# The skip term of eight tiles by VectorE into PSUM, identity or addition chosen per state tile, and a new order list

## The chip, the core and the metric

The kernel runs on one core of a Trainium2 chip. The metric is the device time of one execution in microseconds (us), lower is better; several runs are made and their median is given. The engines are named as in the profile: PE is TensorE (PEld its weight loads), DVE is VectorE, ACT is ScalarE, POOL is GpSimd, and SP (SyncE) issues DMA transfers.

## The reference

Two branches over the same 2048 rows of 512 columns are mixed by a gate g per row, g = sigmoid(sum(x * gate_w)):

```python
# branch a: a diagonal complex state-space scan, with a skip term
Bu = einsum("bld,pd->blp", x, B_bar)
for t in range(L): h = Lam_bar * h + Bu[:, t, :]
a = 2.0 * einsum("blp,dp->bld", hseq, Cmat).real + x * Dskip
# branch b: linear attention, 32 heads of 16, softmax(+) and softmax(-) features
num = phi_q @ (phi_k^T v);  den = phi_q @ sum(phi_k) + 1e-6
b = (num / den) @ wo
out = g * a + (1 - g) * b
```

The skip term x * Dskip is an elementwise product: a row of x times one vector of 512 numbers.

## The kernel before

The 2048 rows are split by residue modulo 8: row number = (a * 128 + c) * 8 + r, with r from 0 to 7, two halves a, and 128 rows c. So there are 16 output tiles of 128 rows, numbered ti = 2r + a; the list `order` has tile n of the output loop take r in the order 7, 1, 3, 5, 0, 2, 4, 6. x stands transposed in SBUF (`xT`), loaded by DMA transposes.

The stages are small generators, and every `yield` ends one step. A list, `ORDER`, written out by hand or by a planner, names the steps in the order in which they are issued, and PE, DVE, ACT and SP keep that order. A token is a stage with a tile number (`y4`), with `@` the PSUM banks it takes, with `:D` that its PSUM copy or scaling goes to DVE instead of ACT, with `:A` that its store is issued by ACT instead of SP. POOL is not in that manual schedule. Its instructions follow in program order, each behind its own waits.

The stages that matter here:

- `k`, `v`, `q` (L477 to L491): projections of x, by products on PE at L475, copied to SBUF by `evac` (L119 on ACT, L121 on DVE).
- `x`, `n`, `e`, `s` (features of k; `X`, `N`, `E`, `S` for groups 1 to 3 of q, `xA` to `sA` for group 0): trees of maxima and minima on DVE (L511, L521, L527), exponentials on ACT (L138), sums on DVE, a factor `rho`, and DMA transposes from SP into `phT` (L563).
- `g` (L597): products of x with B, 256 columns each (L601), and with powers of the decay (L606, L608), copied to `uv`.
- `z` and `h` (L622, L660): the scan over 256 chunks gives the state at r = 7 (`H7`); `st_h(r, j)` makes the states of the other r for state tile j (four tiles). There `dg` times the earlier state goes into PSUM (L668), and `uv` is added in one of two ways: by a product with the identity into the same bank (L667) and a copy by `evac`, or by an addition on DVE out of PSUM (L672). Which one is set by `H_VECTOR`, L54: r = 1, 2, 4, 5, 6 are added on DVE, r = 0 and 3 by the identity.
- `c` (L586 to L619): the scaled output matrices `C2r`, `C2i`, of which `phT0` is the scratch.
- `y` (L711): for one output tile, eight products of 512 columns with C2 (L717, four per step), then four products of 128 columns with a diagonal matrix `Dd` that holds Dskip (L722). They stay in one PSUM bank, `py`.
- `o` (L725): attention for one tile: products `pn` (L736), logarithm and copy `nu`, `rd` on ACT, the product `on` on DVE (L744), and its transposition to `oT`: by a DMA transpose from SP (L758), or for the last four tiles on PE (L753).
- `t` (L761): four products with Wo into the same bank `py` (L765), the scaling by the gate into `ot` (L769 on ACT, L771 on DVE), and the store (L773).

`END` (L696) closes the memory pools of the first part and opens those of the last.

Of the kernel before, what the change touches and what calls it, by code (L numbers as in the profile page):

```python
# [23 lines left out]
ORDER = """
NR F:28 NI B W1@0 W0@1 W0 W2@2 W1:D W3@3 W3 f1@4 W2:D f0@5 f2@6 f0 f1:D l10 V@0 F:4 V P f3@1 f3 f2:D F:4 P P k1@2 k1
l13 P2 k0@3 P2 U P2 P2 P2 P2 P4 k2@4 P3 P3 k3@5 P4 P4 k0 v0@0 i0 i2 U i0 i0 i1 i2 k4@7 i0:D i0 k2 i2 i2:D i2 U k3 k5@6
i1 v3@1 n0 x0 l9 i1 V2@2 i3 l12 x0 k4 v2@3 i3 i3 l14 i1 k5 n0 x0 n0 x0 i3 k7@4 n0 x0 U n0 i1 l11 k6@5 n1 x1 x1 n1 x1
n1 l8 R0 R1 x1 i3 k7 M v7@7 x1 n1 n1 k6:D L V2 v1@6 x2 n2 e0 v6@4 v5@5 v4@2 e0 x2 s0 v0 l15 n2 s0 n2 v2 s0 v1 R2 s0 v6
v3 n2 k10@0 k10 s0 k9@3 k9 C4 k13@6 gw D R3 s0 k12@4 e1 v7 s0 e1 s1 C6 k11@1 k11 x2 s1 k14@0 k8@3 k12 k14 k8 v4 k13
a0@71 a0 x2 s1 x2 s1 v5 g00@4 g00 g60@0 n2 x3 s1 g20@3 g60 s1 g10@2 g10 n3 e2 g30@6 g40@5 g10 s1 a1 x3 g20 n3 a1 x3 n3  # L30
x3 g41@4 n3 C3 e2 e2 e2 x3 g30 g40 g30 k15@0 k15 n3 e3 s2 x4 s2 x4 g01@2 g01 e3 e3 s2 g50@3 g11@5 g50 s2 s2 s2 n4 x4
n4 Q3 n4 s2 g50 g21@6 e3 s3 v8@0 g31@2 g11 Q2 g11 n4 g70@3 Q1 s3 C7 g21 g70 v9@5 g70 g70 z0 z0 g31 g31 Q0 w1@6 C0 a2
a2 a2 w0@3 s3 z0 v11@2 v9 g61@5 g41 R4 z0 w1 v8 z0 z0 g61 s3 w2@4 s3 s3 a2 x4 z0 z0 g51@6 g51 x4 w2 C2 s3 w3@0 g51 v11
n4 R5 w3 g71@5 g71 g71 g71 z1 z1 g02@4 g02 g42@6 a3 a3 z0 z0 g42 w0 e4 e4 z1 z1 z1 g62@2 g12@0 q1@5 C1 h50@4 C5 J1 e4
e4 z1 q2@6 q2 g12 g12 g22@3 g22 J0 h50 z1 z1 g62 q3@4 q3 J2 s4 z1 s4 q0@6 z1 s4 q0 q1 xA nA g32@0 J3 g32 g32 h60@3 J0
g52@2 g52 c4 h60 J2 c4 g52 h51@4 c2 s4 s4 g72@6 R7 g72 xA h10@5 nA g72 g72 c2 xA J3 nA h10 v10@0 v10 J1 s4 c5 h51 c5
R6 g23@3 v12@2 c4 c0 c0 g63@5 nA z2 z2 a3 a3 g03@4 xA g03 z2 z2 z2 z2 xA g23 z2 z2 g33@6 c5 v12 z2 z2 g13@0 g13 g63
g43@4 h32@3 g13 nA g43 h52@2 h52 g33 h32 h61@5 h61 h12@0 c0 g53@4 h12 g33 g53 s4 v14@3 c2 eA eA h42@2 h42 g73@6 g53 eA
eA g73 g73 q10@5 sA h11@0 h11 O h00@4 g73 sA v13@2 h00 v13 a4 z3 sA v15@6 z3 v15 h20@0 h01@4 h30@2 v14 h20 sA h30 z3
h31@6 z3 z3 sA a4 h01 h31 c6 c6 sA q13@3 q13 z3 a4 a4 Y Y h22@0 G q10 z3 z3 G q6@2 q6 h22 z3 z3 sA sA Y Y c1 c1 q9@4  # L40
q8@6 q5@7 h62@3 h41@5 c3 h41 c1 c3 c3 h13@0 h62 q11@2 h13 q11 q8 q12@1 c6 q12 h21@5 q5 h21 h02@2 c7 q4@6 q4 h53@3 h53
h23@1 h23 h33@0 h33 sA q9 h40@7 h40 sA q7@5 h43@6 h63@3 c7 h43 q7 c7 y4@0 y4 sA h63 sA h03@1 END h02 o0@4 o0 X1 N1
o1@7 o1 q14@6 X1 N1 h03 o0@5 X1 o1@2 o1 o1 o0 o0 q15@3 o2@4 o2 o2@7 o2 N1 q15 X1 N1 X1 N1 E1 E1 y2@1 y1@2 y1 E1 E1 q14
X2 y0@5 y0 o1 y4 X2 N2 X2 o0 o0 o3@4 o3 o3@7 o3 o1 o3 y2 X2 N2 o2 X2 N2 S1 S1 N2 S1 o3 S1 N2 S1 S1 o3 y5@3 o2 o2 S1 S1
S1 y1 E2 E2 E2 E2 y9@6 G N3 y5 y5 y3@4 y2 X3 X3 N3 t1 G t1 N3 S1 N3 S2 y9 y9 S2 S2 S1 S1 S2 y3 y3 t3 y0 t0 t0 t2 t2
y6@7 X3 t2:A o4@2 o4 o4@5 o4 o4 y6 y6 t3 X3 o4 X3 o4 S2 S2 t3 o5@1 o5 o5@2 o5 o5 y13@5 y13 o5 N3 o6@4 S2 o6 o6@1 o6 o6
y12@2 o5 y7@4 y7 y12 o6 o6 t4 y7 S2 S2 t4:D S2 E3 E3 E3 E3 S2 o7@1 o7 t5 t5 S3 o7@0 o7 S3 o7 t6 S3 o7 S2 o7 y8@1 o8@3
t6 o8 o8@0 o8 o8 S3 S3 y12 t0:A y11@7 o8 o8 o9@3 o9:D o9@0 o9:D S3 y8 y8 o9 o9 S3 S3 o9 o10@3 y11 o10 o10@0 y11 o10
o10 S3 y14@3 S3 y14 t7 t7:D t8 y14 t8 y15@0 o11@4 S3 o11 o11@1 t9 o12@4 o11:D o11 S3 o10 o10 o12 o12@1 o12 o12 t9:D
o11 y15 o13@4 o13:D o13@6 t6:A o13 o13 o11 o12 y10@1 o14@4 y15 o14:D o12@6 t9 o12:D t7:A t1 y10 y10 o13 o15@4 o15  # L50
o15@6 t4:A t5 o15 o15 t8 o15 t12 t12 t12:A t10 o14@4 o14 o14 t10:D o13@6 t11 o15@2 o15 t10 o13:D t11 t11:A y13 t13 o14
o14@1 t15 t15 t15 o14:D t14 t13 t13 t14 t14:A
"""
# [15 lines left out]
def kernel(  # L69
# [589 lines left out]

    def st_h(r, j):  # L660
        ph = bank([P, 2, NC], F32, "ph")
        add = (r, j) in H_VECTOR
        for h in range(2):
            t = 2 * j + h
            src = hs(r - 1, t, slice(0, NC)) if r in (2, 4, 6) else hs(7, t, slice(-1, NC - 1))
            if not add:
                MM(out=ph[:, h, :], lhsT=ident[:], rhs=uv[j][:, r, h, :], start=(h == 0), stop=False, skip_group_check=True)  # L667
            MM(out=ph[:, h, :], lhsT=dg[:, (r + 1) // 2 if r % 2 else 0, t, :], rhs=src, start=(add and h == 0), stop=True, skip_group_check=True)  # L668
        yield
        dst = HM[:, 2 * j:2 * j + 2, (r - 1) // 2, :] if r % 2 else HE[r // 2][:, 2 * j:2 * j + 2, :]  # L670
        if add:
            VT(out=dst, in0=ph[:], in1=uv[j][:, r], op=ALU.add)  # L672
# [38 lines left out]
    def st_y(n):  # L711
        ti = order[n]
        r, a = ti // 2, ti % 2
        py = bank([P, D], F32, "py")
        live["py", n] = py
        for t in range(NT2):
            MM(out=py[:], lhsT=hs(r, t, slice(a * P, (a + 1) * P)), rhs=C2B[t], start=(t == 0), stop=False)  # L717
            if t % 4 == 3:
                yield
        for kt in range(KT):  # L720
            xs = xT[:, kt, ti * P:(ti + 1) * P]
            MM(out=py[:, kt * P:(kt + 1) * P], lhsT=xs, rhs=Dd[:, kt, :], start=False, stop=False)  # L722
# [38 lines left out]
    def st_t(n):  # L761
        ti = order[n]
        py, oT = live["py", n], live["oT", n]
        for g in range(HG):
            MM(out=py[:], lhsT=oT[:, g, :], rhs=Wo[:, g, :], start=False, stop=(g == HG - 1))  # L765
        yield
        ot = pools["op"][1].tile([P, D], BF16, name="ot", bufs=14)
        if sel["eng"] == "act":
            nc.scalar.mul(out=ot[:], in_=py[:], mul=G[:, ti:ti + 1])  # L769
        else:  # L770
            VS(out=ot[:], in0=py[:], scalar1=G[:, ti:ti + 1], scalar2=None, op0=ALU.mult)  # L771
# [76 lines left out]
```

## Time and profile before

| | before |
|---|---|
| median of 3 runs (lowest to highest) | 155.52 us (155.03 to 155.8) |
| profiled execution, first to last instruction (the one time that the page gives for it) | 153.2 us |
| PE busy | 146.2 us (95%) |
| DVE busy | 132.4 us (86%) |
| ACT busy | 129.2 us (84%) |
| POOL busy | 15.8 us (10%) |
| bytes moved by DMA | 17.55 MB |

Busy time is the union of an engine's instructions. Rows of groups read: line, engine, operation, output and inputs, shape, count, then busy us, mean ns of one, and idle us ahead of the group with what ended it. Rows of stages read: stretch, length, then busy us and count for PE, PEld, DVE, ACT and POOL, the granted clock, the DMA share (1 is all 16 DMA engines), GB/s. Rows of the timeline read: start, length, engine, line, operation, with `x` and a count where equal instructions are merged. Rows of waits read: who waited, for whom, us in total, times, longest. DMA rows end in the median us from issue to landing.

### The profile page before, as it was taken

How to read it: one execution, taken by the hardware profiler on the slowest of the kernel's cores; microseconds unless marked ns; L12 is line 12 of the kernel's file. 1: busy time of each engine (PE TensorE's matmuls, PEld its weight loads, DVE VectorE, ACT ScalarE, POOL GpSimd, SP SyncE). 2: the span in 40 equal slices, each digit the busy share in tenths (PEclk: the TensorE clock that was granted, in tenths of full speed). 3: DMA queues.
4: the chain of work that ended last, by engine and by line, in shares of the span. 5: the costliest groups of instructions: out<-in, count | busy, mean ns of one | idle time of the engine just before them, and what ended most of it. 6: DMA issues, size and time to landing. Idle time of an engine off the chain costs nothing.

```text
span 153.2 us, 3361 instructions
## 1 busy us (share of the span) xinstructions
PE 146.2 (95%) x1236; PEld 95.0 (62%) x1254; DVE 132.4 (86%) x303; ACT 129.2 (84%) x279; POOL 15.8 (10%) x43
## 2 busy tenths in 40 slices
PE   7899999999999999999999999999999999999990
PEld 7644434788878985869867656555554455555540
DVE  3799999999999999999999999999999958717520
ACT  3489998999998999999998999699498998627562
POOL 8239980000000000000000000000000000000000
PEclk9999999999999999999999999999999999999997
DMA  4875995534445699930000007711278859969842
GB/s 116 164 218 97 223 178 112 103 75 103 103 107 78 129 230 178 166 115 4 0 0 4 0 0 169 74 37 34 42 98 147 176 122 189 162 129 206 247 143 103
DMA packets 50848, 17.55 MB, mean 115 GB/s; under 512 B 44176, under 2 KB 50832, under 8 KB 50832
## 3 DMA queue, kind: packets, MB, share of 16 engines
q1 hardware_dynamic: 48976, 15.75, 53.8%
q10 hardware_dynamic: 1696, 1.57, 3.2%
q8 instruction: 10, 0.16, 0.5%
q0 software_dynamic: 160, 0.01, 0.2%
q14 instruction: 6, 0.05, 0.1%
HBM read 2.64 MB, written 2.10 MB: 31 GB/s over the span
## 4 chain that ended last, share of the span: by engine, by line
PE 78%; SPq 10%; DMA 7%; issue 1%; ACT 1%
PE pgq L601 18%; PE py L717 16%; PE pq L475 9%; PE py L765 8%; SPq L229 8%; PE pv L475 4%; PE ph L668 4%; PE pk L475 4%; DMA xT<-in_A_x_dram 4%; PE kvacc L578 3%; DMA phT<-EEq 3%; PE pn L736 3%; PE pgq L606 2%; PE py L722 2%; PE pgq L608 2%; SPq L284 1%
## 5 line engine op out<-in xcount | busy, mean ns | idle before, releaser
L601 PE MATMUL pgq<-xT,BT 128*128 128x256 bf16 x256 | 31.5, 272 | 0.0
L475 PEld LDWEIGHTS <-xT 128*128 128x128 bf16 x192 | 18.2, 98 | 18.3 <-DMA xT<-in_A_x_dram 0.7
L601 PEld LDWEIGHTS <-BT 128*128 128x128 bf16 x256 | 24.6, 98 | 4.1
L138 ACT ACTIVATE EEk<-EEk 128x1024 bf16<-128x1024 bf16 x20 | 20.4, 1080 | 0.0
L119 ACT CAST uv<-pgq 128x512 bf16<-128x512 f32 x28 | 15.9, 605 | 0.5 <-PE pgq L601 0.4
L475 PE MATMUL pv<-Wv,xT 128*128 128x512 bf16 x59 | 15.5, 379 | 0.3
L475 PE MATMUL pq<-Wq,xT 128*128 128x512 bf16 x60 | 15.4, 379 | 0.2
L765 PE MATMUL py<-Wo,oT 128*128 128x512 bf16 x62 | 15.3, 379 | 0.1
L475 PE MATMUL pk<-Wk,xT 128*128 128x512 bf16 x62 | 14.7, 379 | 0.3 <-DMA xT<-in_A_x_dram 0.2
L138 ACT ACTIVATE EEq<-EEq 128x1024 bf16<-128x1024 bf16 x12 | 11.7, 1042 | 0.3 <-DVE EEq L527 0.3
L769 ACT ACTIVATE ot<-py,G 128x512 bf16<-128x512 f32 x12 | 7.9, 686 | 4.5 <-PE py L765 4.3
L138 ACT ACTIVATE ld<-pn 128x16 f32<-128x16 f32 x32 | 6.1, 191 | 5.7 <-PE pn L736 4.6
L590 ACT ACTIVATE phT<-X,dgB 128x512 bf16<-128x512 bf16 x16 | 10.7, 725 | 0.0
L119 ACT CAST nu<-pn 128x256 bf16<-128x256 f32 x27 | 9.9, 380 | 0.0
L119 ACT CAST vx<-pv 128x512 bf16<-128x512 f32 x16 | 9.1, 604 | 0.4 <-PE pv L475 0.4
L548 DVE TENSOR_TENSOR EEk<-EEk,rck 128x4096 bf16<-128x4096 bf16 (+1 forms) x5 | 9.3, 1858 | 0.0
L744 DVE TENSOR_TENSOR on<-nu,rd 128x512 bf16<-128x512 bf16 x16 | 6.7, 421 | 2.8 <-ACT rd L138 1.6
L765 PEld LDWEIGHTS <-oT 128*128 128x128 bf16 x64 | 5.7, 97 | 5.3 <-DMA oT<-on 0.5
L119 ACT CAST Xq<-pq 128x512 bf16<-128x512 f32 x16 | 8.9, 608 | 0.0
L119 ACT CAST Xq<-pk 128x512 bf16<-128x512 f32 x15 | 8.6, 598 | 0.4 <-PE pk L475 0.4
L736 PEld LDWEIGHTS <-phT 128*128 128x128 bf16 x128 | 6.2, 97 | 3.8 <-DMA phT<-EEq 1.4
L511 DVE TENSOR_TENSOR smk<-smk 128x512 bf16<-128x512 bf16 (+4 forms) x18 | 8.1, 448 | 0.1
(178 smaller groups left out, 321.2 us busy)
## 6 DMA issues: line engine op xcount, KB each, us to landing
X<-HM SPq DMA_DIRECT2D x8, 256.0 KB, 4.5
out_dram<-ot ACTq DMA_DIRECT2D x8, 128.0 KB, 2.5
out_dram<-ot SPq DMA_DIRECT2D x8, 128.0 KB, 2.2
C2r<-in_B_wqkv_dram ACTq DMA_DIRECT2D x2, 256.0 KB, 3.8
Wv<-in_B_wqkv_dram SPq DMA_DIRECT2D x1, 512.0 KB, 4.0
Bn<-in_A_B_re_dram SPq DMA_DIRECT2D x1, 512.0 KB, 5.7
Bn<-in_A_B_im_dram SPq DMA_DIRECT2D x1, 512.0 KB, 6.8
Wo<-in_B_wo_dram SPq DMA_DIRECT2D x1, 512.0 KB, 4.3
```

What stands on the lines that cost most here:

```text
L119: nc.scalar.copy(out=out_ap, in_=in_ap)
L138: ins = nc.scalar.activation(**kw)
L229: nc.sync.dma_start_transpose(out=xT[:, :, ti * P:(ti + 1) * P], in_=x_res[ti // 2, ti % 2])
L475: MM(out=pt[:], lhsT=xT[:, kt, ti * P:(ti + 1) * P], rhs=W[:, kt, :], start=(kt == 0), stop=(kt == KT - 1))
L511: VT(out=dst, in0=cur[:, :, :, 0:n, :], in1=cur[:, :, :, n:2 * n, :], op=op)
L548: VT(out=E5, in0=E5, in1=rc.to_broadcast([P, L, 2 * NB, Dh, 4]), op=ALU.mult)
L590: nc.scalar.mul(out=t_, in_=x_, mul=c_)
L601: MM(out=pg[:, h, :], lhsT=BT[:, kt, 2 * j + h, :], rhs=xT[:, kt, r * NC:(r + 1) * NC], start=(h == 0 and kt == 0), stop=(r % 2 == 0 and k ...
L717: MM(out=py[:], lhsT=hs(r, t, slice(a * P, (a + 1) * P)), rhs=C2B[t], start=(t == 0), stop=False)
L736: MM(out=pn[:, 4 * m:4 * m + 4, :].rearrange("p h e -> p (h e)"), lhsT=ph[:, 4 * hf + m, :], rhs=KVm[:, 4 * hf + m, :], start=(m == 0), st ...
L765: MM(out=py[:], lhsT=oT[:, g, :], rhs=Wo[:, g, :], start=False, stop=(g == HG - 1))
L769: nc.scalar.mul(out=ot[:], in_=py[:], mul=G[:, ti:ti + 1])
```

## The change

Four things are changed.

1. For eight of the 16 tiles (n = 6, 8 and 10 to 15) the four products with `Dd` go. Instead DVE multiplies rows of x by Dskip into the PSUM bank `py`, ahead of the tile's products, and the products with C2 add onto it. The other eight (`SKIP_PE`) keep the products with `Dd`, now ahead of those with C2.
2. A new step `XL` loads what DVE needs: x in row layout, all r but 7, as two DMAs (one for each half a) of 128 x 7,168 bytes, and Dskip broadcast to 128 partitions. All three are issued by POOL. To make room the output buffers `ot` go from 14 to 8.
3. Identity or addition in `st_h` is chosen per state tile (r, j): 11 of 28 by the identity where it was 8.
4. `ORDER` is new from the first banks on: the steps up to the first key features stand in the same order on other banks, and the later list is another one. Counted over all of it, DVE does four more `ot`, one more `uv` copy and one `nu` less, and ACT the reverse.

```diff
-H_VECTOR = tuple((r, j) for r in (1, 2, 4, 5, 6) for j in range(4))
+H_IDENT = ((0, 1), (1, 3), (2, 3), (3, 0), (3, 1), (3, 2), (3, 3), (4, 0), (4, 1), (4, 3), (6, 3))
+SKIP_PE = (0, 1, 2, 3, 4, 5, 7, 9)
...
-        add = (r, j) in H_VECTOR
+        add = (r, j) not in H_IDENT
...
+        enter("xp", name="xrows", bufs=1)
+    def st_XL():
+        xp = pools["xp"][1]
+        xr = xp.tile([P, 2, NR - 1, D], BF16, name="xr")
+        dr = xp.tile([P, D], BF16, name="dr")
+        live["xr"], live["dr"] = xr, dr
+        rows = x2.rearrange("(a c r) d -> c a r d", r=NR, c=P)
+        for a in range(2):
+            nc.gpsimd.dma_start(out=xr[:, a], in_=rows[:, a, 0:NR - 1])
+        nc.gpsimd.dma_start(out=dr[:], in_=A_Dskip.unsqueeze(0).to_broadcast([P, D]))
         yield
...
         py = bank([P, D], F32, "py")
         live["py", n] = py
+        if n in SKIP_PE:
+            for kt in range(KT):
+                MM(out=py[:, kt * P:(kt + 1) * P], lhsT=xT[:, kt, ti * P:(ti + 1) * P], rhs=Dd[:, kt, :], start=(kt == 0), stop=False, skip_group_check=True)
+        else:
+            VT(out=py[:], in0=live["xr"][:, a, r, :], in1=live["dr"][:], op=ALU.mult)
+        yield
         for t in range(NT2):
-            MM(out=py[:], lhsT=hs(r, t, slice(a * P, (a + 1) * P)), rhs=C2B[t], start=(t == 0), stop=False)
+            MM(out=py[:], lhsT=hs(r, t, slice(a * P, (a + 1) * P)), rhs=C2B[t], start=False, stop=False, skip_group_check=True)
             if t % 4 == 3:
                 yield
-        for kt in range(KT):
-            xs = xT[:, kt, ti * P:(ti + 1) * P]
-            MM(out=py[:, kt * P:(kt + 1) * P], lhsT=xs, rhs=Dd[:, kt, :], start=False, stop=False)
-        yield
...
-        ot = pools["op"][1].tile([P, D], BF16, name="ot", bufs=14)
+        ot = pools["op"][1].tile([P, D], BF16, name="ot", bufs=8)
```

More of the change, by code (lines that the diff above doesn't have):

```diff
@@ L24 @@
 ORDER = """
[L25 to L49, printed above, removed]
@@ L50 @@
-o11 y15 o13@4 o13:D o13@6 t6:A o13 o13 o11 o12 y10@1 o14@4 y15 o14:D o12@6 t9 o12:D t7:A t1 y10 y10 o13 o15@4 o15
-o15@6 t4:A t5 o15 o15 t8 o15 t12 t12 t12:A t10 o14@4 o14 o14 t10:D o13@6 t11 o15@2 o15 t10 o13:D t11 t11:A y13 t13 o14
-o14@1 t15 t15 t15 o14:D t14 t13 t13 t14 t14:A
+NR F:28 NI B W1@1 W0@2 W0 W2@3 W1:D W3@4 W3 f1@1 W2:D f0@2 f2@3 f0 f1:D l10 V@4 F:4 V P f3@2 f3 f2:D F:4 P P k1@1 k1
+l13 P2 k0@2 P2 U P2 P2 P2 P2 P4 k2@1 P3 P3 k3@3 P4 P4 k0 v0@0 i0 i2 U i0 i0 i1 i2 k4@2 i0:D i0 k2 i2 i2:D i2 U k3 k5@1
@@ new lines @@
+i1 v3@4 n0 x0 l9 i1 V2@5 i3 l12 x0 k4 v2@3 i3 i3 l14 i1 k5 n0 x0 n0 x0 i3 k7@2 n0 x0 U n0 i1 l11 k6@1 n1 x1 x1 n1 x1
+n1 l8 R0 R1 x1 i3 k7 M v7@6 x1 n1 n1 k6:D L V2 v1@2 x2 n2 e0 v6@1 v5@5 v4@7 e0 x2 s0 v0 l15 n2 s0 n2 v2 s0 v1 R2 s0 v6
+v3 n2 k10@0 k10 s0 k9@1 k9 C4 k13@0 gw D R3 s0 k12@1 e1 v7 s0 e1 s1 C6 k11@4 k11 x2 s1 k14@6 k8@2 k12 k14 k8 v4 k13 s1
+a0@41 a0 s1 x2 g20@6 g00@7 Q0 s1 x2 C2 g20 C0 g00 s1 n2 n3 e2 x3 g40@0 k15@7 s1 Q1 g60@6 g40 g10@0 C1 e2 J1 a1 e2 a1
+g60 e2 n3 x3 J1 g41@2 x3 n3 x3 x3 k15 g01@6 n3 g10 n3 v5 g10 s2 Q2 g30@3 g21@5 g30 g41 n4 s2 v8@2 s2 e3 g50@0 s2 g30
@@ new lines @@
+g50 e3 s2 Q3 x4 s2 n4 R4 g11@3 g50:D R5 g70@7 g01 g11 s2 x4 e3 g70 C7 g51@0 e3 C5 n4 g21 g31@5 g11 C3 s3 w1@3 s3 g61@6
+g31 g70 x4 g70 w1 a2 g61 a2 a2 x4 s3 z0 J2 s3 g31 w3@5 w2@6 g51 s3 w3 v8 g51 a2 w0@5 g02@3 n4 z0 w2 g71@0 z0 s3 z0 R6
+z0 x4 w0 g02 g71 g71 g71 n4 q1@5 q2@3 v10@0 e4 q2 q1 s3 e4 v9@6 e4 v9 J0 z1 J3 J2 z1 e4 g22@3 q3@5 z1 q3 z0 a3 v10
+g12@2 z1 z1 a3 g32@6 g12 q0@5 c2 g22 z0 g42@0 z0 g12 q0 c3 z1 z0 g42 J3 z0 z1 s4 z1 h10@2 s4 z1 g62@3 J0 h00@5 c2 c3
+h50@7 h10 s4 g32 nA g32 v11@0 a3 s4 v11 z1 g52@2 xA xA c5 c4 g52 R7 xA a3 h51@0 c5 h00 g52 nA g03@5 xA g62 xA g72@6
@@ new lines @@
+h50 g72 g03 s4 g43@5 h11@7 c4 nA c5 nA h51 g72 g72 g13@3 c2 h61@0 s4 nA h61 z2 v14@6 z2 g13 g43 c4 g23@0 eA eA z2 z2
+g23 h11 g63@5 z2 g63 g53@2 eA g33@0 g13 c1 z2 g73@5 z2 v14 g33 z2 z2 z2 g33 q10@3 q12@6 g53 eA s4 h12@0 h01@7 q10
+q13@3 g53 sA h02@2 q12 g73 sA h12 h01 h60@7 g73 g73 v15@6 h02 sA v13@2 c3 c0 sA c1 h60 sA v15 h20@5 v12@0 O q7@7 z3
+v12 h20 h32@6 q5@0 sA a4 z3 c6 h31@5 z3 c0 z3 z3 z3 h32 q6@6 sA v13 c0 z3 sA h31 a4 a4 q7 q6 h22@5 z3 z3 z3 h30@7 c6
+c1 a4 h30 q4@6 G h33@7 h22 h52@2 q13 sA h13@3 q11@5 Y c7 Y h33 Y h13 h53@3 h43@7 Y c7 h42@1 h52 q5 q4 h62@2 h03@0 c6
@@ new lines @@
+sA h53 c7 h23@3 h40@6 h63@4 h43 h21@7 h23 h40 sA q8@3 h41@6 h03 q11 h42 h62 h21 y0@7 h63 q9@4 h41 sA END G o1@6 y4@5
+o0@2 o2@1 X1 y1@0 X1 o1 o1@6 y4 y1 o2 N1 o0 o0@2 q8 o1 o3@6 N1 o2@1 N1 N1 X1 X1 o1 X1 q9 N1 o1 o0 y0 o0 G E1 N2 E1 E1
+o0 E1 XL X2 y0 o1 o2 G o3 q14@4 o3@2 o3 X2 o2 q15@3 X2 X2 X2 o0 y1 N2 S1 y4 S1 t1 y2@2 t0 y2 y9@6 q15 o2 o3 S1 S1 S1
+N2 y3@3 y2 o2 y9 y3 t2 o3 N2 S1 t1 S1 y3 q14 N2 E2 S1 N3 E2 X3 y6@4 o3 S1 t3 E2 S1 y6 E2 N3 X3 t0 y6 S1 o4@1 y12@0 t2
+S2 S1 o4 S2 o4@2 y9 N3 o4 o5@1 S2 y5@7 o4 o5 S2 o5@2 o5 y12 N3 X3 o4 o6@2 S2 o5 X3 X3 S2 o5 o6 o6@1 o4 t2:A S2 y5 o6
@@ new lines @@
+N3 y7@2 o6 y5 t3 o7@1 o7 y7 o5 o6 E3 S2 t4 y13@3 E3 y12 o6 E3 o7@1 t5 S2 t4:D y8@5 o7 t0:A o7 t3 t5:D y13 t6 y11@7 E3
+y13 S3 o8@1 o8 t6 S2 y8 t1 S2 o8@1 o7 y11 o8 o9@1 o8 o9 S2 y8 S3 S3 o8 o7 S3 o9@1 S3 o8 y7 y14@4 o9:D o10@1 S3 y11 y14
+o9 o9 S3 S3 o10:D t7 o11@1 t8 o11:D t8 o10@1 o9 S3 y14 t4:A t6:A o10 t9 t7:D o11@5 y15@2 S3 o10 t9:D o11 o11 y15 o12@5
+o12 o12@1 S3 o10 y15 o12 o11 y10@6 o12 S3 o12 o13@5 o13 o13@1 y10 o13 o12@5 o10 o14@1 o11 y10 o13 o12:D o14 o14@1
+o15@5 t12 o13 o15 o15@5 t10 t7:A o15:D o14 o15 t12:D o13@1 t5 o14 o15 o14 o13 t12:A t8 t11 o15@1 o14@5 t13 t11 t9
@@ L53 @@
+t11:A o15:D t15 t10:D o14:D t10 t15:D t13:D t14 t15 t13 t14 t14:A
 """
-H_VECTOR = tuple((r, j) for r in (1, 2, 4, 5, 6) for j in range(4))
+H_IDENT = ((0, 1), (1, 3), (2, 3), (3, 0), (3, 1), (3, 2), (3, 3), (4, 0), (4, 1), (4, 3), (6, 3))
 OT_PE = (12, 13, 14, 15)
+SKIP_PE = (0, 1, 2, 3, 4, 5, 7, 9)
 SPIN_BANK = 7
@@ L715, in st_y @@
         live["py", n] = py
+        if n in SKIP_PE:
[3 more added lines that the diff above has]
+            VT(out=py[:], in0=live["xr"][:, a, r, :], in1=live["dr"][:], op=ALU.mult)
+        yield
         for t in range(NT2):
-            MM(out=py[:], lhsT=hs(r, t, slice(a * P, (a + 1) * P)), rhs=C2B[t], start=(t == 0), stop=False)
+            MM(out=py[:], lhsT=hs(r, t, slice(a * P, (a + 1) * P)), rhs=C2B[t], start=False, stop=False, skip_group_check=True)
             if t % 4 == 3:
                 yield
-        for kt in range(KT):
-            xs = xT[:, kt, ti * P:(ti + 1) * P]
-            MM(out=py[:, kt * P:(kt + 1) * P], lhsT=xs, rhs=Dd[:, kt, :], start=False, stop=False)
-        yield
     def st_o(n):
@@ L764, in st_t @@
         for g in range(HG):
-            MM(out=py[:], lhsT=oT[:, g, :], rhs=Wo[:, g, :], start=False, stop=(g == HG - 1))
+            MM(out=py[:], lhsT=oT[:, g, :], rhs=Wo[:, g, :], start=False, stop=(g == HG - 1), skip_group_check=True)
         yield
-        ot = pools["op"][1].tile([P, D], BF16, name="ot", bufs=14)
+        ot = pools["op"][1].tile([P, D], BF16, name="ot", bufs=8)
         if sel["eng"] == "act":
@@ L778 @@
     st = {"V": st_V(), "V2": st_V2(), "U": st_U(), "P": st_P(), "P2": st_P2(), "P3": st_P3(), "P4": st_P4(), "B": st_B(), "gw": st_gw(),
-          "M": st_M(), "D": st_D(), "L": st_L(), "G": st_G(), "Y": st_Y(), "END": st_END(), "NR": st_N(0), "NI": st_N(1), "O": st_O()}
+          "M": st_M(), "D": st_D(), "L": st_L(), "G": st_G(), "Y": st_Y(), "END": st_END(), "NR": st_N(0), "NI": st_N(1), "O": st_O(), "XL": st_XL()}
     for n in range(8, NTI):
@@ L814 @@
         next(st[tok])
-    for key in ("op", "fq", "eq", "sq"):
+    for key in ("xp", "op", "fq", "eq", "sq"):
         pools[key][0].__exit__(None, None, None)
```

## The prediction

> **What bounds the kernel now.** I read the page's totals first, then the stages, then who kept TensorE waiting, then the chain that ended last.
>
> ```profile
> PE 146.2 (95%) x1236; PEld 95.0 (62%) x1254; DVE 132.4 (86%) x303; ACT 129.2 (84%) x279; POOL 15.8 (10%) x43
> ```
>
> ```profile
> 90.00:100.00 10.00, 9.89 (x74) 6.27 (x75) 10.00 (x22) 8.66 (x19) 0.00 (x0) 1.00 0.57 94
> 110.00:120.00 10.00, 9.95 (x76) 5.33 (x75) 9.60 (x21) 8.44 (x18) 0.00 (x0) 1.00 0.78 119
> 120.00:130.00 10.00, 9.71 (x71) 4.96 (x72) 7.59 (x12) 9.17 (x26) 0.00 (x0) 1.00 0.80 159
> 130.00:140.00 10.00, 9.95 (x90) 5.50 (x90) 5.44 (x11) 5.27 (x21) 0.00 (x0) 1.00 0.90 157
> 140.00:150.00 10.00, 9.06 (x78) 4.98 (x76) 4.30 (x10) 6.45 (x19) 0.00 (x0) 1.00 0.69 190
> ```
>
> ```profile
> PE pn L736 <- DMA phT<-EEq: 0.2, 1, 0.2
> PE pk L475 <- DMA xT<-in_A_x_dram: 0.2, 1, 0.2
> ```
>
> The stages give length, then busy time of PE, PEld, DVE, ACT, POOL, the granted clock, the DMA share and GB/s. PE is full in every stage (9.7 to 9.95 of 10), at a granted clock of 1.00. After the first x tiles it waits for others only 0.2 us, twice. DVE is just as full at 90 to 100 and nearly so to 120, and then falls to 7.6, 5.4 and 4.3 of 10. So the end is set by the length of the PE stream; DVE is a second bound up to about 120 us, and spare afterwards.
>
> ```profile
> 148.34 0.89 ACT ot L769 x2
> 149.23 0.27 issue
> 149.50 0.69 ACT ot L769
> ```
>
> That is the end of the chain: behind the last product come one scaling and its store. The page gives 153.2 us for the profiled execution from first to last instruction; the median of the runs is 155.52, so 2.3 us lie around the span. A change of the span is carried to the median one for one.
>
> **PE's sum.** Durations of products overlap, so the spacing of starts counts. Four Dskip products and four identity or state products:
>
> ```profile
> 109.59 0.22 PE py L722 x4
> ```
>
> ```profile
> 98.02 0.27 PE L667 MATMUL ph<-uv,ident 128*128 128x256 bf16 x1
> 98.13 0.27 PE L668 MATMUL ph<-H,dg 128*128 128x256 bf16 x1
> ```
>
> Eight tiles lose their four 128-column products: 8 x 0.22 = 1.76 us of the path. Identity instead of addition now serves 11 state tiles where it served 8 (all of r=0 and r=3): 3 tiles x 2 products x 0.11 = 0.66 us more. All other products are the same. Net -1.10 us. In the eight tiles that keep PE, the Dskip products come first instead of last: same work.
>
> **The other engines.**
>
> ```profile
> L672 DVE TENSOR_TENSOR Bn<-ph,uv 128x512 bf16<-128x512 f32 x8 | 5.4, 684 | 0.0
> L594 DVE TENSOR_TENSOR C2i<-phT 128x512 bf16<-128x512 bf16 x4 | 1.7, 418 | 0.0
> L121 DVE CAST Wk<-pf 128x512 bf16<-128x512 f32 x2 | 1.4, 686 | 0.0
> L771 DVE TENSOR_SCALAR ot<-py,G 128x512 bf16<-128x512 f32 x4 | 3.0, 750 | 4.2 <-PE py L765 4.1
> L121 DVE CAST nu<-pn 128x256 bf16<-128x256 f32 x5 | 2.0, 423 | 2.6 <-ACT ld L138 2.6
> L769 ACT ACTIVATE ot<-py,G 128x512 bf16<-128x512 f32 x12 | 7.9, 686 | 4.5 <-PE py L765 4.3
> L119 ACT CAST HM<-ph 128x512 bf16<-128x512 f32 x4 | 2.4, 588 | 0.1
> ```
>
> A bf16 multiplication from SBUF into PSUM does not occur in the trace. Between 0.418 (all operands bf16 in SBUF) and 0.750 (the dearest group with a 512-wide PSUM operand) I take 0.684, the two-operand group with 32-bit PSUM on one side: 8 x 0.684 = 5.5 us (3.3 to 6.0). Up to the query features DVE loses 3 x 0.684 and gains one uv copy, 0.686: -1.37. Afterwards it gains 5.5, four more ot (3.0), and loses one nu (0.42): +8.05. In 120 to 150 us it has 30 - 7.59 - 5.44 - 4.30 = 12.7 us free, and two of the multiplications lie earlier. They fit, though each stands in DVE's queue ahead of feature work, and four wait there for an ot that frees their bank. ACT: 3 x 0.588 more, four ot, one uv copy less, one nu more: about -1.2. The queues get shorter where they are full.
>
> **The load of x rows** is new: POOL issues two loads of 128 x 7,168 B each and a broadcast of Dskip, 1.97 MB in all.
>
> ```profile
> Wv<-in_B_wqkv_dram SPq DMA_DIRECT2D x1, 512.0 KB, 4.0
> oT<-on SPq DMA_TRANSPOSE x12, 2.6
> phT<-EEk SPq DMA_TRANSPOSE x4, 2.8
> ```
>
> ```profile
> 90.82 7.83 SPq L563 DMA_TRANSPOSE phT<-EEk  x4
> ```
>
> ```profile
> 112.97 0.68 DVE L511 TENSOR_TENSOR mnq<-Xq 128x1024 bf16<-128x1024 bf16 x1
> 113.57 0.68 DVE L511 TENSOR_TENSOR mxq<-Xq 128x1024 bf16<-128x1024 bf16 x1
> ```
>
> ```profile
> 102.00:104.00 2.00, 2.00 (x11) 0.90 (x10) 2.00 (x5) 1.74 (x4) 0.00 (x0) 1.00 0.00 0
> 114.00:116.00 2.00, 2.00 (x13) 1.06 (x13) 1.93 (x7) 2.00 (x4) 0.00 (x0) 1.00 1.14 67
> 116.00:118.00 2.00, 2.00 (x18) 0.95 (x17) 1.90 (x4) 1.43 (x5) 0.00 (x0) 1.00 0.99 198
> ```
>
> By the built order the load waits for the four phT<-EEk transposes, whose source lies in that memory. The last is issued about 97.4 (90.82 + 7.83 less one issue of some 1.25) and lands 2.8 later; less DVE's 1.37 that is 99. The first multiplication (y6) stands behind the two rows at 112.97 and 113.57, so at about 114.2 - 1.4 = 112.8, and needs the first load and the broadcast, which is queued last. At 198 GB/s (the 116 row) 1.97 MB take 10 us and land at 109; at Wv's 0.524 MB in 4.0 us they take 15 and land at 114. I take 10: the DMA engines are idle at 102 to 104. Where 15 holds, DVE stands 1 to 2 us with the last features behind it.
>
> POOL's own speed beside a busy DVE has rows too:
>
> ```profile
> 1.96 0.77 POOL L251 DMA_DIRECT2D vec_n<-in_A_Lambda_im_dram  x1
> 11.82 1.18 POOL L392 TENSOR_TENSOR dl<-ssm_par 128x4 f32<-128x4 f32 x1
> 14.15 0.19 POOL L389 TENSOR_TENSOR dl<-ssm_par 128x4 f32<-128x4 f32 x1
> ```
>
> Beside DVE one small operation takes 1.18 us and a like one 0.19: POOL can be stretched sixfold. Three issues of 0.77 us would then be 14 us instead of 2.3, and the loads 12 us late. The Trainium skill, "SBUF — State Buffer", section "SBUF: two separate sides", warns of this: descriptors of a POOL DMA cannot be written while DVE holds the shared port pair. By that rule the sum would end on the slow side. Its section "Who interferes with whom" narrows it: two-input DVE operations hold up POOL's reads, not its descriptor writing; by that reading the sum stands. No row here shows a POOL DMA beside two-input DVE work. DVE's work at 97 to 113 is nearly all of two inputs, and the 0.77 us came with DVE in use, so I leave the issue at 0.77.
>
> **The list anew.** Much is moved. What I checked is work ahead of a landmark, counted by rows.
>
> ```profile
> 103.33 0.42 DVE L744 TENSOR_TENSOR on<-nu,rd 128x512 bf16<-128x512 bf16 x1
> ```
>
> ```profile
> 110.73 1.03 PE L765 MATMUL py<-Wo,oT 128*128 128x512 bf16 x4
> ```
>
> ```profile
> 101.11 4.32 PE py L717 x20
> ```
>
> Before the first Wo product the new order has six groups of four C2 products fewer (4.32 / 5 = 0.86 each) and one Dskip group fewer, but the 0.66 us of identity: 110.73 - 5.2 - 0.2 + 0.7 = 106.0. The first `on` comes 1.37 earlier, and 0.60 more because one tree step goes behind it: it ends at 103.33 + 0.42 - 1.97 = 101.8, and its transpose lands 2.6 later, at 104.4. The lead shrinks from 110.73 - 103.75 - 2.6 = 4.4 us to 1.6, and this transpose shares the DMA engines with the x load. Each of the first four oT has such a lead. The order is tighter, not looser. On the other side PE's 0.2 us wait on phT may go. I enter 0 for the list, from -0.5 (the small gaps gone) to +1.5 (leads overrun).
>
> **Sum:** 155.52 - 1.10 = 154.4 us, span 152.1.
>
> **Rivals.** *No change, 155.2 (154.8 to 156.2):* the 1.1 us turn into waits. DVE and ACT are full to 115, and PE now asks earlier; 0.8 us of overrun leads is enough. For it: DVE at 10.00 of 10. Against: DVE's own queue ahead of the features is 1.37 shorter, more than PE gains there.
>
> *Slower, 157.0:* the x load, beside the oT and phT transposes, reaches into 114 to 118, where the DMA share already is 1.14 and 0.99. The multiplication y6 stands in DVE until about 115.5, 2.7 us late, and the last query group's trees, exponentials and transposes move back with it: 155.5 - 1.1 + 2.7 = 157.1, rounded to 157.0. It decides from a landing later than about 113.5; below that it costs nothing. For it: the saturated rows. Against: the idle row at 102 to 104.
>
> *The load held by DVE, 160 or more:* the sixfold POOL row applied to the issues; up to 12 us late, less the 4 us of slack, is +8 less 1.1: 162.
>
> *Not what it says:* a multiplication that waits for its bank makes PE wait more than the 0.22 it saves. Eight times that is the no-change case, and is counted there.
>
> **Chances.** Forecast 0.57, no change 0.25, load late 0.13, load held 0.05. About 0.5% (0.78 us) is what a measurement of this kernel can tell from no change, so faster is below 154.74: 0.57; same 0.25; slower 0.18. The range goes from 153.5 (small gaps gone, half a microsecond more) to 156.6, into the case of a late load; some 0.05 is left out below and 0.13 above.
>
> **What would show it.** Right: PE still about 9.9 of 10 in every stage, the Dskip group at 32 products, y6's multiplication with no DMA wait, the first `ot` earlier, and the last scaling starting near 148.4 instead of 149.50. Wrong: PE idle put down to oT or phT transposes between 104 and 120, DVE idle put down to the x rows or Dskip, POOL issues of several microseconds, or multiplications far above 0.75 us.

## The result, and the profile after

The changed kernel takes 160.16 us (median) where the kernel before took 155.36 beside it: ratio 1.0307, 95% interval 1.0271 to 1.0343; one of its four executions took 163.66 us, and the ratio leaves it out. The forecast was 154.4. The profiled execution takes 160.3 us, 158.5 of them from first to last instruction (153.2 before).

First the totals and the chain that ended last, from the page of the changed kernel:

```profile
PE 147.3 (93%) x1210; PEld 94.7 (60%) x1228; DVE 140.4 (89%) x312; ACT 128.9 (81%) x278; POOL 17.5 (11%) x46
...
PE 28%; SPq 27%; DVE 25%; DMA 14%; issue 3%; ACT 1%; DVEq 0%; ACTq 0%
```

Before, the chain was PE to 78%. Now PE carries 28% of it, and SP's queue, DVE and DMA carry 66%. DVE gained 8.0 us of busy time (6.7 forecast). Then PE's waits, and the stages in which they fall:

```profile
PE py L780 <- DMA oT<-on: 1.3, 2, 0.7
...
PE pgq L602 <- ACT uv L120: 1.0, 2, 0.6
PE pv L476 <- DVE Xq L122: 0.6, 1, 0.6
PE pn L751 <- DMA phT<-EEq: 0.5, 1, 0.5
...
PE pf L432 <- DMA HM<-in_B_wqkv_dram: 0.2, 1, 0.2
```

```profile
20.00:30.00 10.00, 9.41 (x65) 4.70 (x65) 9.86 (x22) 9.50 (x18) 3.21 (x8) 1.00 0.80 128
30.00:40.00 10.00, 9.57 (x102) 7.99 (x101) 9.59 (x17) 9.42 (x18) 0.00 (x0) 1.00 0.52 92
40.00:50.00 10.00, 9.15 (x89) 7.61 (x89) 9.86 (x17) 9.12 (x18) 0.00 (x0) 1.00 0.67 131
110.00:120.00 10.00, 9.36 (x53) 4.69 (x54) 9.93 (x20) 8.07 (x18) 0.00 (x0) 1.00 0.43 82
```

PE is no longer full: it loses something at 20 to 50 us, where the forecast had not looked, and again from 110 on. The waits on `uv` and `Xq` are copies that free a PSUM bank; those on `oT`, `phT` and `HM` are transposes by DMA. The chain in order of time shows the places (start, length, what):

```profile
42.54 2.30 SPq L293
44.89 3.34 DMA HM<-in_B_wqkv_dram
...
106.11 4.45 DMA oT<-on
...
117.86 4.62 DMA phT<-EEq
```

The first product with Wo, in PE's order (in brackets, how long PE stood idle before it and what ended that):

```profile
110.60 1.04 PE L780 MATMUL py<-Wo,oT 128*128 128x512 bf16 x4 [0.59 <-DMA oT<-on]
```

Here is the reading that matters most. The first product with Wo starts at 110.60; before, it started at 110.73. The forecast had it at 106.0, because some 5 us of products that stood ahead of it now stand behind it. That work is behind it, but the landmark itself did not come earlier. Two things end there at nearly the same time: PE had done the work ahead of it only at 110.0, 4 us late, and `oT` landed at 110.55, so that PE stood idle 0.6 us more.

What was new did almost what was said. The multiplications (min, median, max ns), the issues of the load on POOL, and the landing times at 100 to 112 us:

```profile
L733 DVE TENSOR_TENSOR py<-xr,dr x8: 690/692/700, 117.6 to 144.4; 128x512 f32<-128x512 bf16 x8
```

```profile
L714 POOL DMA_DIRECT2D xr<-in_A_x_dram x2: 547/604/661, 101.6 to 102.2; - x2
```

```profile
xr<-in_A_x_dram POOLq DMA_DIRECT2D x2, 896.0 KB, 6.6
dr<-in_A_Dskip_dram POOLq DMA_DIRECT2D x1, 128.0 KB, 7.2
oT<-on SPq DMA_TRANSPOSE x2, 4.0
```

No wait for the rows or for Dskip is listed. But the two `oT` transposes beside the load took 4.0 us (median), against 2.4 in the kernel before (its row of issues, and the landing times of its first four):

```profile
L758 SPq DMA_TRANSPOSE oT<-on x4: 1189/1190/1262, 105.2 to 111.7; - x4
...
DMA to landing us min/median/max: 2.4/2.4/2.5
```

### The profile page after: what moved, and what is told of

Its sections match the earlier page's. It is cut to its first block, busy times and chain, and to the rows that moved or that the text cites. A ratio compares the mean times of both kernels' runs of the same rounds, so it can differ in the third digit from the quotient of the medians.

```text
span 158.5 us, 3329 instructions
## 1 busy us (share of the span) xinstructions
PE 147.3 (93%) x1210; PEld 94.7 (60%) x1228; DVE 140.4 (89%) x312; ACT 128.9 (81%) x278; POOL 17.5 (11%) x46
## 4 chain that ended last, share of the span: by engine, by line
PE 28%; SPq 27%; DVE 25%; DMA 14%; issue 3%; ACT 1%; DVEq 0%; ACTq 0%
SPq L230 14%; PE py L736 8%; PE py L780 7%; DMA phT<-EEq 6%; DMA oT<-on 5%; SPq L297 4%; PE pgq L602 4%; SPq L293 4%; SPq L289 3%; DVE HM L673 2%; PE pq L476 2%; DMA HM<-in_B_wqkv_dram 2%; DVE smk L512 2%; DVE H L653 2%; DVE w L642 1%
## 5 line engine op out<-in xcount | busy, mean ns | idle before, releaser
L780 PE MATMUL py<-Wo,oT 128*128 128x512 bf16 x63 | 15.9, 379 | 1.4 <-DMA oT<-on 1.3
L120 ACT CAST uv<-pgq 128x512 bf16<-128x512 f32 x27 | 15.3, 597 | 0.1
L591 ACT ACTIVATE phT<-X,dgB 128x512 bf16<-128x512 bf16 x16 | 11.3, 736 | 0.7 <-DMA X<-HM 0.7
L751 PEld LDWEIGHTS <-phT 128*128 128x128 bf16 x128 | 7.0, 98 | 5.8 <-DMA phT<-EEq 1.3
L714 POOL DMA_DIRECT2D xr<-in_A_x_dram x2 | 1.2, 604 | 78.1 <-DMA phT<-EEk 78.1
L120 ACT CAST Xq<-pq 128x512 bf16<-128x512 f32 x16 | 9.4, 610 | 0.0
L784 ACT ACTIVATE ot<-py,G 128x512 bf16<-128x512 f32 x8 | 5.4, 682 | 4.3 <-PE py L780 4.0
L751 PE MATMUL pn<-KVm,phT 128*128 128x68 bf16 x128 | 8.0, 194 | 0.6 <-DMA phT<-EEq 0.5
```

Source lines behind the costliest of these rows:

```text
L120: nc.scalar.copy(out=out_ap, in_=in_ap)
L591: nc.scalar.mul(out=t_, in_=x_, mul=c_)
L751: MM(out=pn[:, 4 * m:4 * m + 4, :].rearrange("p h e -> p (h e)"), lhsT=ph[:, 4 * hf + m, :], rhs=KVm[:, 4 * hf + m, :], start=(m == 0), st ...
```

## The experiments

The theories, as the expectations name them. A: the new list gives a tile the bank that was freed last, and PE waits for the copy that frees it. B: the new order of steps has too short leads. C: the multiplication and the load cost the time. D: SP's queue brings the query weights too late. E: the load slows the first `oT` transposes. F: the first `oT` is a gate, and a wait there lasts to the end. G: behind that gate stand others, in series. A was my first theory, with B and C as its rivals; D to G were formed from the results.

### Banks alone

**e4: the kernel before, each tile on the bank freed last.** Steps and work are untouched.

```diff
-... W2@2 W1:D W3@3 W3 f1@4 ...
+... W2@1 W1:D W3@0 W3 f1@0 ...
```

> The kernel before, all steps in their order; only the bank numbers are dealt again, each tile taking the bank freed last. Theory A (banks): PE waits for the copies that free them, 158 to 161 us. Theories B and C: 155.4, no change, since neither the order of steps nor the work is touched.

231.62 us, ratio 1.4826 (1.4708 to 1.4944). The page and PE's waits:

```profile
PE 167.2 (72%) x1254; PEld 100.9 (44%) x1254; DVE 135.0 (58%) x303; ACT 134.5 (58%) x279; POOL 15.0 (6%) x43
```

```profile
PE pgq L600 <- ACT uv L118: 5.6, 7, 1.2
PE pn L735 <- ACT nu L118: 5.4, 10, 0.6
```

The mechanism of theory A is real, and far dearer than expected: 76 us from bank numbers alone. In the profiled execution PE stands idle 57 us longer than before and is busy 21 us longer, at a mean granted clock of 0.948 instead of 0.995. The Trainium skill, "Perfetto Trace Analysis", section "Matmuls", says that independent groups of products should rotate through the banks, so that the copies out of one overlap the products into the next; this run agrees, with 155.8 us rotated and 231.6 not.

**e1: the changed kernel, each tile on the bank free longest.**

```diff
-... a0@41 a0 s1 x2 g20@6 g00@7 ...
+... a0@07 a0 s1 x2 g20@5 g00@1 ...
```

> The changed kernel with its step order, multiplication and load as they are; only the bank numbers behind @ are dealt again, each tile taking the PSUM bank that has been free longest (the eight multiplied tiles only banks whose last tenant was a full 512-column product). Theory A (banks): the new list gives a tile the bank freed just before, so PE waits for the copy that frees it; then most of the 4.6 us over before goes: 156 to 158 us, with the PE waits on ACT uv and DVE Xq gone. Theory B (the new order of steps has too short leads from product to copy to use): 159.5 to 160.5. Theory C (multiplication and x load take DVE, POOL and DMA time): 159.5 to 160.5.

164.97 us, ratio 1.0544 (1.0443 to 1.0644): slower still, as no theory had it.

```profile
PE pn L750 <- ACT nu L119: 2.5, 5, 0.5
PE pf L431 <- DMA HM<-in_B_wqkv_dram: 1.8, 2, 1.7
```

The waits on `uv` and `Xq` are gone. PE then came to the query weights before they had landed, and at the end other bank waits arose. So the banks are not what holds the changed list up by themselves: what hides behind a bank wait is the next wait.

**e7 and e3: the kernel before with 29 other bank numbers, without and with the multiplication.** The 29 numbers follow a rule: a tile that VectorE starts takes only a bank whose last tenant was a full 512-column product. No run here tests that rule.

```diff
-... y6@7 X3 t2:A o4@2 o4 o4@5 ...
+... y6@2 X3 t2:A o4@7 o4 o4@7 ...
```

> The kernel before with the 29 bank numbers that the run with the multiplication in the list before had, and nothing else: all sixteen tiles multiply by Dskip on TensorE, no rows are loaded. If the bank numbers made that run slow: 160 to 162.5. If the multiplication did, by holding a bank earlier and by its place in VectorE's queue: 155 to 156. Between the two the difference says what each costs.

> The kernel before with its own step order, plus the load of the x rows after the second E1 step and the multiplication on VectorE in the eight tiles; identity or addition as before; of 176 bank numbers 29 change, since a multiplied tile needs a bank whose last tenant was a full 512-column product. Theories A and B: the multiplication by itself does what was forecast, minus 1.8 us, 153.3 to 154.5. Theory C: 157 or more.

e7: 159.23 us, ratio 1.0247 (1.0202 to 1.0291). e3: 162.67 us, 1.0450 (1.0381 to 1.0520). PE's waits, e7 and then e3:

```profile
PE pn L735 <- ACT nu L118: 2.3, 4, 0.7
```

```profile
PE pn L750 <- ACT nu L119: 3.8, 5, 1.4
...
PE py L735 <- DVE py L732: 1.3, 1, 1.3
```

e7 falls between its two cases. e3 is as slow as theory C said (157 or more), but for more than half of it the reason is another: bank numbers cost some 3.8 us, multiplication and load together another 3.4. PE's longer waits for `nu` and for the multiplication fit a simple reading, which no run tests apart: in the old list a multiplied tile holds its bank from the multiplication on, and the attention products wait for a bank.

### The first half of the new list

**e5: the query weights earlier.** Only SP's steps are shown.

```diff
-... Q0 ... C2 ... C0 ... Q1 ... C1 ... J1 ... J1 ... Q2 ... Q3 ...
+... Q0 ... C2 ... C0 ... Q1 ... Q2 Q3 C1 ... J1 ... J1 ...
```

> The changed kernel; only two loads move on SP's queue: the third and fourth transposed loads of the query weights are issued ahead of a load of C and the first two X copies instead of behind them. Theory D (SP's queue): in the changed list they land at 46.5 and 48.2 us, in the list before at 41.0 and 43.6, and TensorE cannot fold the query weights earlier; then they land near 45 and the time falls by 1.5 to 2.5 us, to 157.6 to 158.6. Theories A to C: 159.8 to 160.3, no change, since what they blame is untouched.

159.75 us, ratio 1.0294 (1.0242 to 1.0347): 0.4 us at best, not the 2 of theory D; theories A to C had said no change. No wait for the weights is left, but the others are:

```profile
PE pn L750 <- DMA phT<-EEq: 1.2, 1, 1.2
...
PE pgq L601 <- ACT uv L119: 1.0, 2, 0.6
PE pv L475 <- DVE Xq L121: 0.5, 1, 0.5
```

e1 took the bank waits away and found the weights; e5 took the weights away and kept the bank waits. Neither alone gains.

**e2: the changed list, products kept, no load; e6: the load on SP's queue behind the first two oT.** For e2 `SKIP_PE` holds all 16 tiles and XL goes; for e6 XL stands behind the second `oT`:

```diff
-            nc.gpsimd.dma_start(out=xr[:, a], in_=rows[:, a, 0:NR - 1])
+            nc.sync.dma_start(out=xr[:, a], in_=rows[:, a, 0:NR - 1])
```

> The changed kernel with its list and banks, but all sixteen tiles multiply by Dskip on PE and the x rows are not loaded. Theory C (multiplication and load): the time falls to 156 or less. Theories A and B (banks, order of steps): 160 to 162, as the eight products cost PE up to 1.8 us again and the waits stay.

> The changed kernel; only the load of the x rows and of Dskip moves, from POOL's queue at 102 us to SP's queue behind the first two oT transposes. Theory E (the load shares the DMA engines with those transposes, 4.4 us where it was 2.4): the wait of 0.6 us for oT goes, and what follows from it, 158.8 to 159.5. If the load costs nothing where it was: 160.1. If the multiplications now wait for the rows (landing near 116, first needed at 117.6): 161 or more.

e2's four executions scatter from 159.98 to 164.55 us and give no ratio; e6 has 161.78 (159.74 to 164.13), ratio 1.0361 (1.0282 to 1.0439). Both keep the late query weights, and PE's wait for them differs from run to run: 0.2 us in the profile of the changed kernel, 1.7 at its longest in e1, 2.5 in e6 and 2.9 in e2. Behind the two longest the granted clock falls to 0.51 and 0.50.

So e2 speaks against theory C in spite of the scatter: no execution comes near 156 us, and the lowest, without multiplication and load, is as slow as the changed kernel. e6 leaves theory E open: none of its executions is as low as 158.8 to 159.5, but its multiplications also start later, at 121.0 instead of 117.6. Later tests in the changed list start from e5.

### The gate: e9, e10, e11

Three edits of the kernel before, with no multiplication, no new list, no new bank. e9 moves the first four Wo products, with the last step of their tile `y1`, up by 4.1 us of work; e10 adds only the load; e11 does both.

```diff
-... y5@3 o2 o2 S1 S1 S1 y1 E2 ... X3 X3 N3 t1 ...
+... y1 t1 y5@3 o2 o2 S1 S1 S1 E2 ... X3 X3 N3 ...
```

```diff
-... X1 N1 E1 E1 y2@1 ...
+... X1 N1 E1 E1 XL y2@1 ...
```

For room, e10 and e11 keep `ot` in 8 buffers instead of 14, as the changed kernel does. In the changed kernel the one wait listed for a store of `ot` is 0.3 us on ACT, so nothing listed points to the smaller number.

> The kernel before; one thing moved: the last step of its tile y1 and the first four Wo products stand 21 steps earlier, ahead of y5's first products, as the changed list has its first Wo products ahead of more of the work. TensorE then asks for the first oT about 4.1 us sooner, at 106.6 instead of 110.7; its transpose landed at 109.0. Theory F (the first oT is a gate: TensorE is gapless behind it, so a wait there lasts to the end): 2.4 us slower, 157.8. If such a wait is made up later: 155.4 to 156.

> The kernel before, its list and its banks, plus only the load of the x rows and of Dskip at the place where the changed kernel has it; nothing uses the rows. Theory F: the first oT transposes take some 4.4 us instead of 2.4, land near 111 where TensorE asks at 110.7, and cost 0 to 0.5 us: 155.4 to 155.9. If the load by itself costs what the changed kernel loses (theory C): 158 or more.

> Both of the two edits before on the kernel before: the first Wo products 4.1 us of work earlier, and the load of the x rows beside the oT transposes. Theory F: the wait is 106.6 to about 111, 4.4 us, and the time 159.3 to 160, as slow as the changed kernel, with no multiplication, no new list and no new bank. If the two do not add up: 158 or less.

| | us | ratio (interval) | PE's wait for `oT` at the first Wo product |
|---|---|---|---|
| e9, short lead | 158.09 | 1.0174 (1.0098 to 1.0250) | 2.0 |
| e10, x rows | 156.23 | 1.0060 (1.0028 to 1.0093) | 1.0 |
| e11, both | 161.48 | 1.0392 (1.0332 to 1.0452) | 4.1 |

PE's wait in e9, then e10's landing times of the four `oT` transposes at 100 to 113 us, then e11's wait:

```profile
PE py L764 <- DMA oT<-on: 2.0, 1, 2.0
```

```profile
DMA to landing us min/median/max: 2.5/4.1/6.2
```

```profile
PE py L776 <- DMA oT<-on: 4.1, 1, 4.1
```

Theory F holds in the old list: both edits without anything else of the change make the old kernel as slow as the changed one (and slower than forecast, 159.3 to 160). The load that nobody reads costs 0.9 to 1.0 us: the first `oT` takes 6.2 us instead of 2.4, and the second, which the first Wo product needs, lands at about 112.0 instead of 109.0. The sum is more than its parts (6.3 against 2.9 and 1.0 us). The stages of e11 (the granted clock is the third number from the end) point to the reason:

```profile
108.00:110.00 2.00, 0.00 (x0) 0.00 (x0) 1.97 (x6) 0.60 (x3) 0.00 (x0) 1.00 1.01 335
110.00:112.00 2.00, 0.70 (x2) 0.28 (x3) 1.96 (x5) 0.91 (x3) 0.00 (x0) 0.52 0.74 142
114.00:116.00 2.00, 2.00 (x7) 0.62 (x5) 1.93 (x7) 2.00 (x3) 0.00 (x0) 0.50 0.84 159
```

After the long wait PE is granted half its clock for some microseconds: the four Wo products take 1.89 us there, and the next four, at 121.0, take 1.03. e9 has such a stretch too (last section); its two executions without one, by the mean granted clock, take 157.4 and 157.5 us, so the wait of 2.0 us itself is worth some 2.2.

### Taking the changed kernel apart: e8, e14, e13, e12, e15, e16

**e8** has the list before up to END and the changed list behind it (a mixed list), with multiplication and load. **e14** is the same with all products on PE and no load. **e13** is e8 with the eight needed tiles' rows (8 of the 14 row blocks) loaded after the last `g` step, while DMA is idle, into the buffer of B that is free by then. **e12** does that to e5. e8, e13 and e14 keep the identity for r = 0 and 3 as before, and banks are dealt again where the two lists collide.

```diff
-        for a in range(2):
-            nc.gpsimd.dma_start(out=xr[:, a], in_=rows[:, a, 0:NR - 1])
+        nc.gpsimd.dma_start(out=xr[:, 0:4], in_=rows[:, 0, 0:NR - 1:2])
+        nc.gpsimd.dma_start(out=xr[:, 4:7], in_=rows[:, 1, 2:NR - 1:2])
+        nc.gpsimd.dma_start(out=xr[:, 7], in_=rows[:, 0, 5])
```

> A kernel that takes the steps of the list before up to its END step, and from there those of the changed list, with load and multiplication; identity for r=0 and r=3 as before; bank numbers dealt again where the two lists collide. It splits the 4.6 us in two. If the first half of the new list costs them (theory D): 155 to 156.5. If the second half does: 158.5 to 160.

> The kernel with the list before up to END and the changed list behind it (159.2), and now the eight tiles' x rows loaded before 95 us instead of beside the first oT transposes. Its first oT was issued at 104.4 and took 5.4 us; TensorE stood 3.4 us. Theory F alone: that wait shrinks to 0.4 and the time falls to 156.2. Theory G (gates in series: behind the first oT come the features of the next query group from VectorE, which do not come earlier): TensorE waits some 100 products later instead, for phT or for a multiplication, and the time falls only to 158 to 159.

> The same mixed list with no multiplication on VectorE and no x rows loaded: all sixteen tiles multiply by Dskip on TensorE. It says what the multiplication is worth where no load disturbs. If the eight tiles' 1.76 us of products count in full: 1.5 to 1.8 us above the run with the rows early. If VectorE's queue takes it back: equal within 0.7.

> The changed kernel with the query weights' loads moved as in the run that did so (159.75), and the eight needed tiles' rows loaded before 95 us, while the DMA engines are idle, into a buffer that is free by then; Dskip's broadcast likewise. Theory F: the first oT lands in 2.4 us, at 108.3 instead of 109.6 to 110.5, but TensorE asks at about 109.7 there, so only what is left of the wait for oT goes: 159.2 to 159.7. If the load beside the transposes is the main cost in the changed list too: 157.5 or less.

| | us | ratio (interval) |
|---|---|---|
| e14, mixed list, products on PE | 159.13 | 1.0204 (1.0131 to 1.0276) |
| e13, + multiplication, rows early | 157.97 | 1.0119 (1.0047 to 1.0191) |
| e8, + load beside oT instead | 159.18 | 1.0258 (1.0200 to 1.0316) |
| e12, changed list, weights and rows early | 160.09 | 1.0291 (1.0221 to 1.0361) |

PE's wait in e8, then the rows of its `oT` at 100 to 125 us (min, median, max ns, then first and last start), and then PE's waits in e13:

```profile
PE py L779 <- DMA oT<-on: 3.4, 1, 3.4
```

```profile
L779 PE MATMUL py<-Wo,oT x16: 379/379/391, 109.8 to 118.1; 128*128 128x512 bf16 x16
L772 SPq DMA_TRANSPOSE oT<-on x6: 1189/1208/1261, 104.4 to 123.8; - x6
...
DMA to landing us min/median/max: 2.4/2.5/5.4
```

```profile
PE pn L750 <- DMA phT<-EEq: 0.9, 1, 0.9
PE py L730 <- ACT nu L119: 0.6, 2, 0.4
PE py L735 <- DVE py L732: 0.6, 1, 0.6
...
PE py L779 <- DMA oT<-on: 0.5, 1, 0.5
```

In e8 PE has one long wait, 3.4 us for the first `oT`; its first Wo product starts at 109.8, so it asked at 106.4, near the 106.0 of the forecast (without the 0.7 us of new identity products, which e8 does not have, the forecast's sum gives 105.3). In e13 the wait is 0.5, yet of its 2.9 us only 1.2 (by the times) to 2.2 (by the ratios) come out: PE waits for `phT`, for a bank and for a multiplication a little later. That fits theory G. e14, without any multiplication or load, stands still too:

```profile
PE pn L750 <- DMA phT<-EEq: 1.2, 1, 1.2
...
PE py L730 <- ACT nu L119: 0.8, 2, 0.5
PE py L779 <- DMA oT<-on: 0.6, 2, 0.4
```

So the new second half by itself, on banks that fit it, is some 3 us slower than the old list. The multiplication takes 1.2 of that back (e14 and e13 ran side by side, and their times do not overlap), between the two cases expected. The load beside `oT` gives 1.2 to 2.2 away again (by the times, by the ratios). Some 0.6 of it goes with a lower granted clock in two of e8's four executions (last section).

e12 misses both of its cases: in the changed list the rows loaded early gain nothing (160.09 against e5's 159.75). Its `oT` landed in 2.4 us, at 108.5, but PE came to the first Wo product only at 109.68.

**e15** asks for the multiplication's worth in the changed list (e5 with `SKIP_PE` holding all tiles, no XL), **e16** is a try at a faster version: a few steps of e13 moved.

```diff
-... S2 t4 y13@3 ... S2 y8 t1 S2 ...
+... S2 y13@3 t4 ... S2 y8 S2 ... S3 t1 ...
```

> The changed kernel with the query weights' loads moved (159.75), and all sixteen tiles' Dskip products on TensorE, no rows loaded. The same question in the changed list: 161.5 if the 1.76 us count in full, 159.5 to 160.3 if they do not.

> The mixed list with the rows early, and a few steps of its second half moved by one to twenty places (t1 and t3 later, y5 and y13 earlier) and two banks swapped, so that fewer waits remain. A try at a version that beats both kernels: 155 to 157.5 where theory G holds; below 155.2 it would beat the kernel before.

e15: 160.84 us, ratio 1.0290 (1.0198 to 1.0381). By the times that is 1.1 above e5, by the ratios nothing: what the multiplication is worth there stays open. But e15 shows what the list, with its banks and its identity products, costs by itself: with no multiplication, no load and no late weights it is some 4.5 us above the kernel before. e16: 158.66 us, 1.0163 (1.0089 to 1.0237), no better than e13. No version here beats the kernel before.

What the new first half costs depends on what stands behind it: 0.6 to 1.0 us with the load beside `oT` (e5 and the changed kernel against e8), 1.3 to 1.7 without multiplication and load (e15 against e14), 2.1 to 2.7 with the rows early (e12 against e13). The traces fit: in e13 PE is at the first Wo product at 106.3 and waits 0.5; in e12 it is there at 109.7. In the changed kernel both the late PE and the late `oT` hold this product at 110, and taking away one leaves the other.

## Why the prediction was wrong

**What bounds the kernel.** Right for the kernel before, though the row for 140 to 150 has 9.06 of 10, outside the 9.7 to 9.95 that the text states for every stage. PE waited for almost nothing there, and e9 shows that a wait of 2 us at 107 us is not made up.

**PE's sum, -1.10 us.** The counts hold, and the eight tiles' 1.76 us were worth about 1.2 where nothing else disturbed (e13 against e14). The rest, 0.6 us, is what e13 lists as PE's wait for `DVE py`.

**The multiplication.** 0.684 taken, 0.692 measured; no wait for its rows is listed. It fits into DVE's spare time after 120 us.

**The load.** Near in itself: issues of 0.55 to 0.66 us (0.77 taken), landing at 110.0 (109 forecast). In part this is luck: it began at 101.6 instead of 99 and took 8.4 us instead of 10. Both rivals on it fall, the late load and the load held by DVE; the second has the nearest time (160 or more) by a mechanism that did not occur. Its pair of POOL rows could not show it either: DVE was busy beside both. The Trainium skill, "SBUF — State Buffer", section "Who interferes with whom", had the narrower reading, and the trace agrees: 547 to 661 ns an issue beside two-input work on DVE. But its price was looked for in the wrong place, at y6's multiplication, which came only at 117.6. It fell on the two `oT` transposes beside it. The text named that ("shares the DMA engines with the x load") and put no number on it.

**The list anew: here the forecast failed.** It was entered as 0, from -0.5 to +1.5, and it is worth some 4.5 us (e15; 4.2 by e2's lowest execution against the 155.79 beside it). Step by step:

- PE's arrival at the first Wo product, 106.0: 110.0 in the changed kernel. The count of the work ahead of it was good within about 1 us (106.4 in e8, behind the old first half), but work ahead of one landmark was all that was counted, and not the waits in the stretch before END. There SP's order had the last query weights issued at 44.89 (40.92 before), and bank reuse put waits at 20, 34 and 46 us. Together the waits listed ahead of the landmark make some 2 of these 4 us.
- The first `oT`, 104.4: wrong by 6.2 us; it landed at 110.55. DVE was to be 1.37 us earlier and was 2.2 later: it began the first query tree at 100.10 instead of 97.91 (first two rows), the tree took 0.7 us longer, and `on` ended at 106.08 (third row) instead of 101.8. The transpose was issued at once, at 106.11, and took 4.45 us beside the load, where 2.6 were taken.

```profile
97.91 0.68 DVE L511 TENSOR_TENSOR mxq<-Xq 128x1024 bf16<-128x1024 bf16 x1
```

```profile
100.10 0.68 DVE L512 TENSOR_TENSOR mxq<-Xq 128x1024 bf16<-128x1024 bf16 x1
...
105.66 0.42 DVE L759 TENSOR_TENSOR on<-nu,rd 128x512 bf16<-128x512 bf16 x1
```

- The lead of 4.4 us in the kernel before was misread. It was reckoned from the end of `on`, 103.75. But the first Wo product belongs to tile 1, and in SP's order the transpose of tile 1 stands behind that of tile 0: it was issued at 106.49 and landed at about 109.0, a lead of 1.7. e9's wait of 2.0 us is that lead overrun.

```profile
106.49 1.26 SPq L758 DMA_TRANSPOSE oT<-on  x1
```

- So the new lead was not 1.6 us but -0.6 in the changed kernel, where PE itself is late, and -3.4 in e8, where it is not. A gate that comes late shifts what is behind it; the bound "+1.5" had no row behind it.

The rival "no change" named the mechanism, overrun leads, at 0.8 us and a chance of a quarter; its size was the mistake. "Not what it says" was right on one point: in e13 PE waits 0.6 us for a multiplication.

**The lesson in e5, e1, e12 and e13.** Removing one kind of wait moved the time by less than the wait (e13), by nothing clear (e5, e12), or up (e1). That fits a list with many gates at nearly the same time, where three engines are full: only the latest shows in the profile.

**What stays open.** How the 3 us of the second half split between step order and bank numbers, since a list cannot be run without banks; what in the first half (order, banks, the new choice of identity) makes PE 4 us and DVE 3.5 us later than counted; and the multiplication's worth in the changed list (e15).
